# Fused RWKV-5 attention and SwiGLU block: spreading feed-forward pieces over the last attention steps, and one later silu product

## The chip, the core and the metric

The kernel runs on one core of one Trainium2 chip. The metric is the device time of one execution in microseconds (us). A run's time is that of the whole execution; the profile's span runs from the first to the last instruction.

## The reference, cut to what matters

```python
# attention: B, H, S, D = 4, 8, 768, 48
for t in range(S):
    cur = einsum('bhd,bhe->bhde', u * k[t], v[t])
    y[:, :, t] = einsum('bhd,bhde->bhe', r[t], state + cur)
    state = w * state + einsum('bhd,bhe->bhde', k[t], v[t])
x = y.transpose(0, 2, 1, 3).reshape(3072, 384)
# feed-forward: d_model 384, d_ff 1536
g = x @ w_gate
val = x @ w_val
out = (g / (1 + exp(-g)) * val) @ w_out
```

Everything is float32.

## The kernel before, in words

**Attention steps.** The 768 positions of each of 4 batches are cut into 6 chunks of 128, which makes N = 24 attention steps. Step `s` of the main loop (L1049) prepares block s and finishes older ones. `scale_k`, `scale_r` and `own_product` run on GpSimd. `move_blocks(s + 1)` puts 16 DMAs of 32 KB on SP's queue (L364), which permute the 32x32 blocks of the next step's keys and rows. `turn_blocks(s)` transposes what such DMAs brought, with two stream transposes on VectorE (L379, kT and rT). `scores(s - 1)` is 16 matmuls (L393) whose results VectorE copies through a mask (L398, two copies, the second put off in `lazy`). `outputs(s - 2)` is 56 matmuls (L426) and a copy on ScalarE (L430), and `update(s - 2)` is 32 matmuls (L441) and two sums on VectorE (L453). From step 12 on scores, outputs and update stand one after the other. In even steps from 14 to 22 `scale_r(s + 1)` comes only after `turn_blocks(s)`.

**Feed-forward pieces.** The feed-forward work of pairs of token blocks is queued in `todo` as closures, "pieces", and `feed(n)` takes n of them. `gaps(s, n)` is called at five places of each step, n = 0 to 4 (before the scores, after the attention matmuls, after the turn, near the end, at the end), and decides how many pieces go there; `turn_blocks` feeds one more between its two transposes, which `gaps` takes off at n = 1. Every engine works its instructions off in program order. So the position of a piece fixes what stands in front of what in the queue of TensorE, VectorE, ScalarE, GpSimd and SP.

**The passes of 3x3 products.** The gate and value products of g = 2, 4, 6 are made by `three_beside(g)` beside attention, in a fast multiplication scheme that works on three feature blocks at a time. There are four triples, t = 0 to 3. Each has 15 rounds of matmuls (L720, four matmul records each in the profile), which write PSUM chains named n, y, l4, l5, l1, l2, l8. Only four PSUM banks exist for them, so a round that reuses a chain waits until ScalarE or VectorE has read it (copies and sums recorded at L744). Its 60 rounds, with all that follows them on other engines, are cut into 26 pieces: the first three hold one round, the others about two and a half. When a triple is complete its silu is made: an activation on ScalarE (L751), then a product with the values, for feature blocks 0 and 1 on VectorE and for block 2 on GpSimd (all L744). `at` numbers say when: z = 15 t is the triple's first round, so z + 16.2 is just after round 1 of the next triple, and z + 22.1 just after its round 7. The values of triples 0, 2 and 3 lie in the same rows of `hv` (`place`), those of triple 1 in others. The last pieces of a pass overlap with `two_projections`, 14 items that multiply by w_out in seven products of quarters (L539, `project`), with sums on VectorE (`h_sums`, L512 to L516).

After the loop the passes for g = 8 and 10 run without attention (`three_units`, L854), and then their projections.

Of the kernel before, what the change touches and what calls it, by code (L numbers as in the profile page):

```python
# [22 lines left out]
def fast(  # L23
# [68 lines left out]
    def take():  # L92
        return free.popleft()
# [130 lines left out]
    def round_weights():  # L224
        if done["act"] > done["pool"]:
            round_pool()
        round_act()
# [390 lines left out]
    def in_place(t):  # L618

        f = 3 * t  # L620
        w = [[wgv[:, :, c, P * (f + i) : P * (f + i + 1)] for c in range(CC)] for i in range(3)]
        return [
            lambda o=o, x=x, op=op: op(o, o, x) for o, x, op in (
                (w[1][1], w[0][1], pool.tensor_add), (w[1][1], w[1][2], pool.tensor_sub),
                (w[0][0], w[1][0], pool.tensor_add), (w[0][0], w[0][2], pool.tensor_sub),
                (w[2][2], w[2][0], pool.tensor_sub), (w[2][2], w[1][2], pool.tensor_sub),
            )
        ]

    def w_forms(g, t):  # L630

        f = 3 * t
        made = wide["u", g, t] = {}

        w = [[wgv[:, :, c, P * (f + i) : P * (f + i + 1)] for c in range(CC)] for i in range(3)]
        def place():
            if t == 0 or g < THREES:
                ring = three.tile([P, 6, 2, P], FP32, name="s", tag="w_bits")
                s = [ring[:, n] for n in range(6)]
            else:  # L640
                s = (early + spare)[6 * t - 6 : 6 * t]
                s = [x.rearrange("p (o t) -> p o t", o=2) for x in s]
            made.update(zip(("r2", "r3", "r13", "r11", "r5", "r9"), s))
            made.update({
                "r0": w[1][1], "r1": w[0][1], "r4": w[0][0], "r6": w[1][2], "r7": w[2][2],
                "r8": w[1][0], "r10": w[2][0], "r12": w[0][2], "r14": w[2][1],
            })

        def form(o, a, b, op):
            op(made[o], made[a], made[b])  # L650

        return [place] + [
            lambda x=x: form(*x) for x in (
                ("r2", "r14", "r6", pool.tensor_sub), ("r3", "r8", "r1", pool.tensor_sub),
                ("r13", "r12", "r10", pool.tensor_add), ("r9", "r2", "r13", pool.tensor_sub),
                ("r9", "r9", "r7", pool.tensor_sub), ("r5", "r3", "r13", pool.tensor_sub),
                ("r5", "r5", "r4", pool.tensor_sub), ("r11", "r3", "r2", pool.tensor_sub),
                ("r11", "r11", "r0", pool.tensor_add),
            )
        ]  # L660
# [49 lines left out]
    def three_step(g, t, n, rounds, open_):  # L710

        what, chain = rounds[n]
        names = [c for _, c in rounds]
        first = n == names.index(chain)
        if first:
            wide[chain] = open_(chain)
        u, v = wide["u", min(g, THREES), t][what], wide["v", g][what]
        ps = wide[chain][:].rearrange("p (o i t) -> p o i t", o=2, i=2)
        for o in range(2):
            pe.matmul(  # L720
                ps[:, o], u[:, o], v,
                start=first and o == 0, stop=True, skip_group_check=True,
            )
# [11 lines left out]
    def three_beside(g):  # L735

        todo = []
# [4 lines left out]
        def later(at, do, out, *args):  # L742
            def run():
                do(out, *(pair_of(wide[a][:]) if isinstance(a, str) else a for a in args))  # L744
            todo.append((at, run))

        def give(at, chain):
            todo.append((at, lambda: free.append(wide.pop(chain))))

        def silu(at, then, gate, value, on):  # L750
            todo.append((at, lambda: act.activation(gate, gate, AF.Silu)))  # L751
            later(then, on.tensor_mul, gate, gate, value)

        for t in range(4):
            z = 15 * t
            rounds = ENDING if t == 3 else BESIDE
            at = {what: z + n + 0.5 for n, (what, _) in enumerate(rounds)}
            for n in range(15):
                todo.append((
                    z + n,  # L760
                    lambda t=t, n=n, r=rounds: three_step(g, t, n, r, lambda _: take()),
                ))
            if t < 3:
                forms = w_forms(g, t + 1)
                if g == FIRST and t < 2:
                    forms += in_place(t + 2)
                start = z - 4 if t else 0
                todo += [
                    (start + (z + 10 - start) * n / len(forms) + 0.15, do)
                    for n, do in enumerate(forms)  # L770
                ]
            place = NR + (6 if t == 1 else 0)
            values = hv[:, place : place + 6].rearrange("p (j i) t -> p j i t", j=2)
            gates = [[j * FC + 3 * t + i for i in range(3)] for j in range(2)]
            c = []
            for k in range(6):
                i, j = divmod(k, 2)
                row, other = gates[j][i], place + 3 * j + i
                low, high = hv[:, row], hv[:, other]
                c.append(bass.AP(  # L780
                    tensor=low.tensor, offset=low.offset,
                    ap=[list(low.ap[0]), [high.offset - low.offset, 2], [1, 2 * P]],
                ))
            later(at["r10"], act.copy, c[5], "n")
            later(at["r14"], act.copy, c[4], "y")
            later(at["r12"], act.copy, c[0], "l4")
            later(at["r13"], dve.tensor_add, c[4], c[4], "n")
            later(at["r2"], dve.tensor_add, c[5], c[5], "y")
            later(at["r9"], dve.tensor_sub, c[4], c[4], "l4")
            give(at["r9"] + 0.1, "l4")  # L790
            later(at["r5"], act.copy, c[1], "n")
            later(at["r5"] + 0.1, dve.tensor_sub, c[0], c[0], "n")
            give(at["r5"] + 0.2, "n")
            later(at["r11"], act.copy, c[2], "y")
            later(at["r11"] + 0.1, act.copy, c[3], "y")
            give(at["r11"] + 0.2, "y")
            later(at["r6"], dve.tensor_add, c[3], c[3], "l5")
            later(at["r3"], dve.tensor_add, c[2], c[2], "l1")
            later(at["r1"], dve.tensor_add, c[0], c[0], "l2")
            later(at["r7"], dve.tensor_add, c[5], c[5], "l5")  # L800
            give(at["r7"] + 0.1, "l5")
            later(at["r4"], dve.tensor_sub, c[1], "l1", c[1])
            give(at["r4"] + 0.1, "l1")
            later(at["r0"], dve.tensor_sub, c[2], c[2], "l2")
            give(at["r0"] + 0.1, "l2")
            later(at["r8"], dve.tensor_sub, c[1], c[1], "l8")
            later(at["r8"] + 0.1, dve.tensor_add, c[3], c[3], "l8")
            give(at["r8"] + 0.2, "l8")
            if t < 3:
                for i, on in enumerate((dve, dve, pool)):  # L810
                    silu(
                        *((z + 11.7, z + 11.8) if i == 2 else (z + 15.6 + i / 10, z + (22.1 if i and t < 2 else 16.2 + i / 10))),
                        hTs[:, :, 3 * t + i], values[:, :, i], on,
                    )
            else:
                for j in range(2):
                    start = (at["r0"] + 0.2, z + 14.8)[j]
                    silu(
                        start, (z + 13.9, 1e9)[j], hTs[:, j, 9:12],
                        values[:, j], dve,  # L820
                    )
# [91 lines left out]
    todo = []  # L913
# [32 lines left out]
    def gaps(s, n):  # L946

        if s not in EARLY:
            if n == 0:
                share[0] = min(-(-len(todo) // (4 - (s - 9) % 4)), 14)  # L950
            feed(share[0] // 5 + (n < share[0] % 5) - (n == 1 and BLOCKS <= s < N))
            return
        for what in EARLY[s][n]:
            if what == "R":
                if done["pool"] < NW:
                    round_weights()
                elif len(summed) < 4:
                    weight_sum()
            else:
                feed(1, 3)  # L960

    share = [0]
# [86 lines left out]
    for s in range(4, N + 2):  # L1049
# [11 lines left out]
        if s < BLOCKS:  # L1061
            turn(s)
        gaps(s, 0)
        if 4 <= s - 1 < N:
            while small:
# [459 lines left out]
```

## Time and profile before

| what | us |
|---|---|
| runs | 608.59, 605.59, 608.40 |
| median of the runs | 608.4 |
| the profiled execution, whole | 605.01 |
| its span | 603.2 |
| TensorE busy | 587.1 |
| VectorE busy | 405.6 |
| GpSimd busy | 313.3 |
| ScalarE busy | 228.2 |

The profiled execution took 1.8 us more than its span and lies 3.4 us under the median of the runs. The granted TensorE clock is 1.000 over the whole span. Busy time of TensorE is an upper bound of its work: matmuls are pipelined, and their ends are modelled. A wait therefore shows best as the time from the start of one row of matmuls to the start of the next, against its usual pace: in this trace 0.216 us for each matmul of L720 and 0.163 us for each of L539.

Scores of the loop's steps 18 to 24 start at 288, 321, 350, 379, 391, 410 and 426 us; the three passes of `three_beside` end at about 219, 311 and 406 us.

### The profile page before, as it was taken

How to read it: one execution, taken by the hardware profiler on the slowest of the kernel's cores; microseconds unless marked ns; L12 is line 12 of the kernel's file. 1: busy time of each engine (PE TensorE's matmuls, PEld its weight loads, DVE VectorE, ACT ScalarE, POOL GpSimd, SP SyncE). 2: the span in 40 equal slices, each digit the busy share in tenths (PEclk: the TensorE clock that was granted, in tenths of full speed). 3: DMA queues.
4: the chain of work that ended last, by engine and by line, in shares of the span. 5: the costliest groups of instructions: out<-in, count | busy, mean ns of one | idle time of the engine just before them, and what ended most of it. 6: DMA issues, size and time to landing. Idle time of an engine off the chain costs nothing.

```text
span 603.2 us, 12420 instructions
## 1 busy us (share of the span) xinstructions
PE 587.1 (97%) x4920; PEld 528.0 (88%) x4920; DVE 405.6 (67%) x682; ACT 228.2 (38%) x524; POOL 313.3 (52%) x349
## 2 busy tenths in 40 slices
PE   8799999999999999999999999989999999999996
PEld 7678888899888889988799988879988899988896
DVE  5867886369478877478877477959347686277660
ACT  3368887331353412253331334523234420243310
POOL 4879889988999402977701967632435200011000
PEclk9999999999999999999999999999999999999999
DMA  7989883231530503133150404121100000000001
GB/s 173 232 213 253 214 300 75 52 64 42 113 49 8 94 4 72 39 64 56 21 89 14 100 2 75 17 45 26 41 14 0 2 1 26 27 1 1 2 1 58
DMA packets 138004, 40.43 MB, mean 67 GB/s; under 512 B 128592, under 2 KB 131792, under 8 KB 137936
## 3 DMA queue, kind: packets, MB, share of 16 engines
q1 hardware_dynamic: 134480, 34.82, 27.3%
q10 hardware_dynamic: 3456, 4.72, 2.2%
q8 instruction: 41, 0.67, 0.5%
q14 instruction: 27, 0.22, 0.1%
HBM read 28.51 MB, written 4.72 MB: 55 GB/s over the span
## 4 chain that ended last, share of the span: by engine, by line
PE 83%; DVE 3%; POOL 3%; SPq 2%; ACT 1%; issue 1%; DMA 1%; DVEq 0%; POOLq 0%; ACTq 0%
PE bank L720 27%; PE bank L539 26%; PE bank L464 7%; PE c_l L720 6%; PE y_ps L426 5%; PE c_n L720 3%; PE c_y L720 3%; PE s_ps L393 3%; DVE hv L744 2%; SPq L364 2%; POOL wgv L222 1%; PE u_ps L441 1%; PE tp L349 1%; DMA r_ld<-in_r_dram 1%; ACT hv L751 0%
## 5 line engine op out<-in xcount | busy, mean ns | idle before, releaser
L744 DVE TENSOR_TENSOR hv<-hv,bank 128x512 f32<-128x512 f32 x132 | 87.2, 682 | 30.5 <-PE bank L720 17.6
L720 PE MATMUL bank<-xf,wgv 128*128 128x256 f32 x256 | 65.9, 381 | 1.7 <-DVE hv L744 1.7
L464 PE MATMUL bank<-xT,wgv 128*128 128x256 f32 x288 | 66.8, 385 | 0.6 <-ACT xT L430 0.6
L860 POOL TENSOR_TENSOR hv<-At,hats 128x512 f32<-128x512 f32 x8 | 10.2, 1274 | 107.0 <-ACT At L859 107.0
L328 ACT ACTIVATE At<-ident,du 128x128 f32<-128x128 f32 x176 | 60.0, 397 | 15.2 <-DVE du L240 8.5
L744 ACT COPY hv<-bank 128x512 f32<-128x512 f32 x72 | 40.2, 585 | 55.2 <-PE bank L720 49.1
L464 PEld LDWEIGHTS bank<-xT,wgv 128*128 128x128 f32 x288 | 53.2, 190 | 8.9 <-ACT xT L430 0.8
L720 PEld LDWEIGHTS bank<-xf,wgv 128*128 128x128 f32 x256 | 48.0, 190 | 8.9 <-DVE hv L744 2.1
L650 POOL TENSOR_TENSOR s<-wgv 128x256 f32<-128x256 f32 x39 | 29.7, 785 | 43.8 <-PE bank L539 43.7
L539 PE MATMUL bank<-wo,hv 128*128 128x192 f32 x288 | 49.5, 327 | 0.0
L539 PEld LDWEIGHTS bank<-wo,hv 128*128 128x128 f32 x288 | 47.3, 190 | 0.5
L398 DVE COPY_PREDICATED At<-mask,s_ps 128x512 f32<-128x512 int32 x48 | 34.2, 743 | 18.4 <-ACT At L328 10.0
L454 POOL TENSOR_TENSOR Z<-Z,w 48x192 f32<-48x192 f32 x32 | 17.3, 539 | 51.2 <-DVE Z L453 50.0
L539 PE MATMUL bank<-wt,hs 128*128 128x192 f32 x240 | 42.1, 328 | 0.7 <-DVE hs L513 0.6
L539 PE MATMUL bank<-wo,hs 128*128 128x192 f32 x240 | 42.4, 326 | 0.0
L545 ACT COPY hv<-bank 128x192 f32<-128x192 f32 x36 | 11.3, 316 | 78.6 <-PE bank L539 78.6
L539 PEld LDWEIGHTS bank<-wt,hs 128*128 128x128 f32 x240 | 39.2, 190 | 1.7 <-issue 1.3
L539 PEld LDWEIGHTS bank<-wo,hs 128*128 128x128 f32 x240 | 39.6, 190 | 0.2
L751 ACT ACTIVATE hv<-hv 128x512 f32<-128x512 f32 (+1 forms) x33 | 21.2, 667 | 47.7 <-DVE hv L744 47.5
L720 PE MATMUL bank<-xT,s 128*128 128x256 f32 x152 | 36.0, 382 | 1.0 <-DVE hv L744 0.7
L426 PE MATMUL y_ps<-At,v_ld 128*32 128x128 f32 x768 | 34.9, 273 | 1.3 <-DVE At L398 1.3
L720 PE MATMUL bank<-xT,wgv 128*128 128x256 f32 x144 | 35.9, 382 | 0.0
(203 smaller groups left out, 1302.4 us busy)
## 6 DMA issues: line engine op xcount, KB each, us to landing
hats<-hats SPq DMA_DIRECT2D x192, 32.0 KB, 2.0
w_bits<-in_moe_w_gate_dram SPq DMA_DIRECT2D x6, 768.0 KB, 6.9
v_ld<-in_v_dram SPq DMA_DIRECT2D x48, 96.0 KB, 3.4
w_bits<-in_moe_w_val_dram SPq DMA_DIRECT2D x6, 768.0 KB, 6.0
w_bits<-in_moe_w_out_dram SPq DMA_DIRECT2D x6, 768.0 KB, 6.4
out_dram<-hv ACTq DMA_DIRECT2D x24, 192.0 KB, 1.9
k_ld<-in_k_dram SPq DMA_DIRECT2D x20, 192.0 KB, 3.3
r_ld<-in_r_dram SPq DMA_DIRECT2D x20, 192.0 KB, 3.8
```

What stands on the lines that cost most here:

```text
L328: lambda h=h: act.activation(At[i % 2][:, h, :], ident[:], AF.Identity, scale=du[:, h : h + 1])
L364: sp.dma_start(out=bass.AP(tensor=dst.tensor, offset=dst.offset, ap=[list(dst.ap[0]), [-P, 2 * HP], [1, 32]],), in_=bass.AP(tensor=src.ten ...
L393: pe.matmul(ps[e][:, a, :], kT[i % 2][rows, at(i, a), :], turned[i][rows, at(i, a), :], start=True, stop=True, skip_group_check=True,)
L398: lazy.append(lambda e=e: dve.copy_predicated(At[i % 2][:].rearrange("p (a e) t -> p a e t", e=2)[:, :, e], mask[:].bitcast(INT32).unsquee ...
L426: pe.matmul(ps[32 * q : 32 * q + 32, cc, :], *x, start=start, stop=stop, skip_group_check=True,)
L454: pool.tensor_mul(ze, ze, w)
L464: pe.matmul(gv[:, o, :].rearrange("p (i t) -> p i t", i=2), wt[:, c, P * f : P * (f + 1)], xT[:, 2 * g % NX : 2 * g % NX + 2, c, :], start ...
L539: pe.matmul(ps, lhs[:, f, :], rhs[:, f, :], start=(f == 0 and n in (0, 1, 4)), stop=(f == FH - 1), skip_group_check=True,)
L650: op(made[o], made[a], made[b])
L720: pe.matmul(ps[:, o], u[:, o], v, start=first and o == 0, stop=True, skip_group_check=True,)
L744: do(out, *(pair_of(wide[a][:]) if isinstance(a, str) else a for a in args))
L751: todo.append((at, lambda: act.activation(gate, gate, AF.Silu)))
```

## The change

Two edits, both in the building of the order; no operation is added or taken away.

```diff
@@ three_beside, silu of triples 0 to 2
-  *((z + 11.7, z + 11.8) if i == 2 else (z + 15.6 + i / 10, z + (22.1 if i and t < 2 else 16.2 + i / 10))),
+  *((z + 11.7, z + 11.8) if i == 2 else (z + 15.6 + i / 10, z + (16.2, 22.1)[i])),
@@ gaps
-  share[0] = min(-(-len(todo) // (4 - (s - 9) % 4)), 14)
+  if s < 18:
+      share[0] = min(-(-len(todo) // (4 - (s - 9) % 4)), 14)
+  else:
+      share[0] = -(-(len(todo) + (14 if s < 21 else 0)) // max(25 - s, 1))
```

The first edit concerns triple 2 alone: its second feature block's product goes from z + 16.3 to z + 22.1, where those of triples 0 and 1 were already. The second changes how many pieces a step gets:

| step s | 18 | 19 | 20 | 21 | 22 | 23 | 24 |
|---|---|---|---|---|---|---|---|
| before | 14 | 14 | 14 | 3 | 7 | 7 | 6 |
| after | 10 | 10 | 10 | 6 | 10 | 10 | 9 |

Steps up to 17 keep theirs. The pieces keep their order among themselves, so what changes is where the attention work of steps 18 to 24 stands between them. Counted along TensorE (r a round, P a projection product, A the attention matmuls of one step), from step 17 to the end of the loop's pieces:

```
before  A17 r18 A18 r17 P r2 P5 A19 P5 r P r P2 r9 A20 r30 A21 r10 A22 r7 P r2 P2 A23 P7 A24 P4
after   A17 r15 A18 r20 P r2 A19 P10 A20 r P r P2 r11 A21 r15 A22 r25 A23 r5 P r2 P6 A24 P7
```

## The prediction

> **What bounds the kernel now.** I read the page first, then a table of windows, then the timelines of TensorE, VectorE, SP and GpSimd around each place where a row of matmuls starts late.
>
> ```profile
> span 603.2 us, 12420 instructions
> ...
> PE 587.1 (97%) x4920; PEld 528.0 (88%) x4920; DVE 405.6 (67%) x682; ACT 228.2 (38%) x524; POOL 313.3 (52%) x349
> ```
>
> TensorE is the bound. The change moves no work off it, so it can only add or remove waits of TensorE. In the part that the change reaches, the windows table leaves little of that:
>
> ```profile
> 196.00:226.00 30.00, 29.24 (x234) 25.58 (x233) 23.79 (x34) 9.75 (x22) 8.20 (x10) 1.00 0.29 49
> 284.00:316.00 32.00, 31.07 (x241) 27.19 (x240) 25.08 (x36) 12.27 (x27) 13.69 (x15) 1.00 0.32 52
> ...
> 378.00:402.00 24.00, 22.28 (x250) 18.66 (x249) 18.24 (x30) 9.27 (x22) 11.41 (x13) 1.00 0.20 31
> ```
>
> (Columns: window, its length, busy time of PE, PEld, DVE, ACT, POOL, clock, DMA share, GB/s.) VectorE, the third figure, is busy for 76 to 79% here. TensorE's timeline shows where it waits; these are the last triples of the three passes:
>
> ```profile
> 203.10 2.11 PE L720 MATMUL bank<-xf,s 128*128 128x256 f32 x8
> 205.07 3.23 PE L720 MATMUL bank<-xT,s 128*128 128x256 f32 x12
> 208.14 1.03 PE L720 MATMUL bank<-sgs,wgv 128*128 128x256 f32 x4
> ...
> 297.40 1.89 PE L720 MATMUL bank<-xf,s 128*128 128x256 f32 x8
> 299.45 1.10 PE L720 MATMUL bank<-xT,s 128*128 128x256 f32 x4 [0.17 <-ACT hv L744]
> 301.28 1.99 PE L720 MATMUL bank<-xT,s 128*128 128x256 f32 x8 [0.73 <-DVE hv L744]
> ...
> 397.58 1.03 PE L720 MATMUL bank<-xf,wgv 128*128 128x256 f32 x4
> 400.33 1.13 PE L720 MATMUL bank<-xf,wgv 128*128 128x256 f32 x4 [1.72 <-DVE hv L744]
> ```
>
> Each start is held against the pace of 0.216 us per matmul. Pass 1: 8 matmuls from 203.10 end at 204.83, the next come at 205.07 (0.24 late); 12 from 205.07 end at 207.66, the next come at 208.14 (0.48). Pass 2: 299.45 is 0.32 late, 301.28 is 0.97 late. Pass 3: 400.33 is 1.89 late. By the same reckoning 390.30 is 0.26 late. At 0.163 us per matmul of L539, 315.21 is 0.19 late, and 224.13 is 0.78 late (for hs, L513). Three more starts after 260 us are about 0.2 late each. What holds TensorE is VectorE's queue:
>
> ```profile
> 202.77 2.88 DVE L744 TENSOR_TENSOR hv<-hv 128x512 f32<-128x512 f32 x2 [0.78 <-ACT hv L751]
> 205.58 1.87 DVE L744 TENSOR_TENSOR hv<-hv,bank 128x512 f32<-128x512 f32 x3
> ...
> 297.07 2.96 DVE L744 TENSOR_TENSOR hv<-hv 128x512 f32<-128x512 f32 x2
> 299.96 0.70 DVE L379 STREAM_TRANSPOSE rT<-hats 128x512 f32<-128x512 f32 x1
> 300.58 1.84 DVE L744 TENSOR_TENSOR hv<-hv,bank 128x512 f32<-128x512 f32 x3
> ...
> 398.99 0.71 DVE L379 STREAM_TRANSPOSE kT<-hats 128x512 f32<-128x512 f32 x1 [1.84 <-DMA hats<-hats]
> 399.62 1.85 DVE L744 TENSOR_TENSOR hv<-hv,bank 128x512 f32<-128x512 f32 x3
> ```
>
> In passes 1 and 2 the two silu products of triple 2 (`hv<-hv`, x2) stand in front of the sums that free chains n and y for rounds r5 and r11. In pass 3 the sums stand behind the transpose of step 22, which waits 1.84 us for its DMAs. These come from one row of SP's queue:
>
> ```profile
> 386.43 10.97 SPq L364 DMA_DIRECT2D hats<-hats  x16
> ```
>
> They start when step 21's transposes end (386.37) and land 2.0 us after the last issue (page, part 6): about 13 us from transpose to transpose. Between them TensorE had step 22's attention and few pieces; step 21 gets 3.
>
> **The change part by part.** Attention of one step costs TensorE 1.09 + 1.68 + 0.41 = 3.2 us (chain; 2.8 without update, from step 22 on), a round 0.863, a projection product 1.95. VectorE pays per step 2 masked copies (0.74), 2 transposes (0.70), 2 sums of L453 (0.35) and a reduction (0.55).
>
> *The moved product, pass 1.* The order around pass 1 is otherwise unchanged. A product took 1.44 us there (2.88 / 2). Without the second, the three sums start at 204.14, the first has read its bank at about 204.8, and r5, due at 205.9, waits for nothing: 0.48 goes. The 0.24 before r9 stays mostly, because ScalarE's copy of l4 overwrites values that the first product reads. I count -0.5. The product now follows r5's sum (208.09 to 208.78). VectorE's gap there is 0.42, and then 0.24, 0.17 and 0.18; a product of 0.69 is absorbed in about four sums. New is a wait on ScalarE: triple 3 writes its values into the rows of triple 2, so r11's two copies (from 208.34) wait for the product, until about 209.5. Behind them is chain y, whose bank is taken again only for r8, seven rounds later, and r3's sum, due at 210.14, to which a copy ending at 210.1 just comes in time. Cost 0. From the other side, up to 0.5 per pass if r4 or r0 slip with the sums; and not a gain, since nothing is taken away there.
>
> *Pass 2, both edits.* Attention 18 moves from four rounds before triple 3 to seven before it. I walk VectorE's queue from the start of A18 = 0. Masked copy 1.3 to 2.05, sums of L453 to 4.1 (as at 289.40 and 291.41 in the trace), the sums of r6, r3, r1 to 6.7, second masked copy 7.4, kT 8.1, r7 and r4 to 9.5, rT 10.2, r0 and two sums of r8 to 12.2. Then the one product left. With 1.48 us, as at 297.07, it ends at 13.7, and ScalarE's l4 copy (0.58) at 14.3. r9 is due at 3.2 + 12 x 0.863 = 13.6 and comes 0.7 late; r5's sum ends at 14.4, before r5 is due. So 1.29 becomes 0.7 (between 0 with an undisturbed product of 0.69, and 1.0). The 0.19 at 315.21 goes too: A19 now stands between round r8 and the products that need hs, which gives VectorE and ScalarE 3.2 us. Sum -0.8.
>
> [...] The row first, min/median/max ns:
>
> ```profile
> L744 DVE TENSOR_TENSOR hv<-hv x24: 677/951/1561, 173.3 to 411.0; 128x512 f32<-128x512 f32 x18, 128x768 f32<-128x768 f32 x6
> ```
>
> Products of 128x512 take 0.69 alone and 1.44 to 1.48 while GpSimd works. [...] I take the row, 1.48. At the product's new place GpSimd is idle in passes 1 and 2 (no GpSimd row from 205.1 to 216.25, nor from 300.9 to 324.9), so both give 0.69.
>
> *Pass 3, the even shares.* Step 21 has 6 pieces, and between A21 and A22 stand 15 rounds, 12.9 us. The same walk from A21 = 0: kT at 4.1, rT ends at 8.2, 16 issues to 19.3, landed at 21.3. kT of step 22 comes up at A22 + 6.9 = 16.1 + 6.9 = 23.0: 1.7 us in time. The stall of 1.89 goes. So does about half of the 0.26, its second product being gone. Steps 18 to 20 are thinned from 14 to 10 pieces, which is still over 20 us each, against 13. Late next is VectorE, since attention now stands right before two triple boundaries. A22 stands after round 13 of triple 1: masked copies, kT, the product (1.04, or 1.48) and rT come before r13's sum, which ends at 10.0 to 10.4 after A22, while r5 is due at 9.8. I take 0.5 (0 to 0.9). A21, two rounds before triple 1: 0.15 (0 to 0.3). At the pass's end A23 no longer stands between r8 and the hs products, as it did at 410 us, so the pattern of 315.21 returns: 0.2 (0 to 0.8, as at 224.13). Sum -1.9 - 0.1 + 0.85 = -1.15.
>
> *Costed at nothing:* ScalarE's diagonals (8 x 0.4 per step, at 38% load), covered by its idle time, at most 0.3 per step without that; the loads of k, r, v on SP behind the 16 DMAs, needed a step later; GpSimd's forms for the pass g = 8, ready 5 us before 439 us in the trace and followed by two more products than needed.
>
> Total -0.5 - 0.8 - 1.15 = -2.45, say -2.5: span 600.7, the profiled execution 605.0 - 2.5 = 602.5. The median of the runs lies 3.4 above the profiled one for no reason that the trace shows, so I carry that over: 608.4 - 2.5 = 605.9.
>
> **The rivals.** *B, everything fits.* VectorE absorbs the moved attention, as it did before around A20 and A21 (345 to 378 us: TensorE 33.0 of 33.0). All the waits named go except the 0.78 at 224.13: 0.72 + 1.29 + 0.19 + 1.89 + 0.26 = 4.35, so 604.0. Against it, VectorE had no slack at the boundaries of passes 2 and 3.
>
> *C, the waits change places.* The upper ends hold: 0.24 and 1.0 stay, 0.9 + 0.3 + 0.26 + 0.8 in pass 3, and 0.5 for the late product in two passes: 4.5 of 4.35 given back. 608.5, no change. The late product's copies on ScalarE speak for it; for the first two triples such a product stood there without a stall.
>
> *D, slower.* The place is step 20. GpSimd's forms for pass 3 wait for the product 06 to free their buffer (before: the idle 5.94 ahead of 332.55). Behind them now queue `scale_k(21)` and `own_product(21)`, four forms, A20's Z products, two forms, and only then `scale_r(21)`, on which SP's 16 DMAs wait. My walk from A20: scale_r ends at 10.3, DMAs land at 23.3, kT of step 21 comes up at 24.4. Slack 1.1 us, and beyond it each us of lateness stalls TensorE by about one us (1.84 gave 1.89). If the nine forms take 1.45 each (the longest seen, at 408.87) instead of 0.78, and the three others 1.5 instead of 1.0, that is 7.5 late, a stall of 6.4 and 605.9 + 6.4 = 612.3. It turns slower than before at 3.6 late. For it: own_product did take 1.46 at 377.63. Against it: GpSimd's mean form is 0.78.
>
> **How the numbers follow.** The likeliest case has 0.60, B 0.18, C 0.15, D 0.07. About 0.5% (3 us) is what a measurement of this kernel can tell from no change. The likeliest case runs from -1.5 to -3.5, so a third of it, 0.22, passes 0.5%; with B that makes faster 0.40, D gives slower 0.07, same is 0.53. The range reaches from 602.0, B less 2.0 because the runs before fell up to 2.8 under their median, to 609.0, C and a little.
>
> **What would show it.** Right: no idle ahead of kT (L379) by DMA; one `hv<-hv` product, not two, ahead of r13's sum in each last triple; TensorE's starts late by under 1 us everywhere from 196 to 440 us, the largest behind A22 and before r9 in pass 2; TensorE's busy work unchanged. Wrong: a wait of L379 for DMA at step 21, a wait of TensorE for ScalarE's r11 copies, or TensorE idle ahead of the pass at 439 us.

## The result, and the profile after

| | before | after |
|---|---|---|
| median of six runs each, one chip | 606.68 us | 602.27 us |
| range of the runs | 605.46 to 608.59 | 602.09 to 603.55 |
| the profiled execution, whole | 605.01 | 602.26 |
| its span | 603.2 | 600.4 |

The kernel became faster: ratio 0.9926, 95% interval [0.9903, 0.9950]. The profiled executions differ by 2.8 us, the medians by 4.4. The runs of before lie in two groups, near 605.5 and near 608; what the upper group is turned out to be the other half of this case. Of the runs below, four single ones took 950 us or more (one of e5, one of e10, two of before); they are in the medians, but in no ratio and no count.

The page of the kernel after, first and second line:

```profile
span 600.4 us, 12410 instructions
...
PE 586.4 (98%) x4920; PEld 528.0 (88%) x4920; DVE 404.7 (67%) x682; ACT 227.8 (38%) x524; POOL 312.7 (52%) x349
```

The 4920 matmul records are the same, busy time moved by under 1 us, and the span fell by 2.8: what went is waiting. The windows table of the kernel after, same stretches and columns as before, shows where:

```profile
196.00:226.00 30.00, 29.37 (x236) 25.96 (x235) 23.87 (x36) 9.84 (x22) 8.18 (x9) 1.00 0.29 50
284.00:316.00 32.00, 32.00 (x334) 28.18 (x333) 24.25 (x38) 13.62 (x31) 14.68 (x17) 1.00 0.39 62
378.00:402.00 24.00, 24.00 (x171) 20.64 (x170) 17.29 (x28) 9.25 (x21) 4.85 (x7) 1.00 0.16 24
```

TensorE, the first figure after the length, is busy for all of the second and third stretch. TensorE's timeline of the kernel after, at the same three places:

```profile
203.19 2.11 PE L720 MATMUL bank<-xf,s 128*128 128x256 f32 x8
205.16 2.83 PE L720 MATMUL bank<-xT,s 128*128 128x256 f32 x12
207.83 1.03 PE L720 MATMUL bank<-sgs,wgv 128*128 128x256 f32 x4
...
297.09 1.98 PE L720 MATMUL bank<-xf,s 128*128 128x256 f32 x8
299.04 2.83 PE L720 MATMUL bank<-xT,s 128*128 128x256 f32 x12
301.70 1.03 PE L720 MATMUL bank<-sgs,wgv 128*128 128x256 f32 x4
...
405.24 4.06 PE L539 MATMUL bank<-wo,hv 128*128 128x192 f32 x24
409.88 2.19 PE L539 MATMUL bank<-wt,hs 128*128 128x192 f32 x12 [0.57 <-DVE hs L513]
```

By the pace of 0.216 us, pass 1 comes 0.24 and 0.08 late (before 0.24 and 0.48), pass 2 comes 0.22 and 0.07 late (before 0.32 and 0.97). The row at 409.88 is new: 24 matmuls at 0.163 us from 405.24 end at 409.15, so TensorE waits 0.73 us for hs, where attention of step 23 used to stand in between. VectorE's timeline of the kernel after:

```profile
296.93 1.29 DVE L744 TENSOR_TENSOR hv<-hv 128x512 f32<-128x512 f32 x1 [0.21 <-ACT hv L751]
298.25 0.69 DVE L744 TENSOR_TENSOR hv<-hv,bank 128x512 f32<-128x512 f32 x1
...
376.24 0.69 DVE L379 STREAM_TRANSPOSE kT<-hats 128x512 f32<-128x512 f32 x1
376.86 0.65 DVE L744 TENSOR_TENSOR hv<-hv 128x512 f32<-128x512 f32 x1
377.43 0.70 DVE L379 STREAM_TRANSPOSE rT<-hats 128x512 f32<-128x512 f32 x1
378.05 1.36 DVE L744 TENSOR_TENSOR hv<-hv,bank 128x512 f32<-128x512 f32 x2
```

One product instead of two stands ahead of the sum at 298.25, and the transpose of step 22 (376.24) no longer waits for DMA. SP's queue shows why:

```profile
361.33 10.76 SPq L364 DMA_DIRECT2D hats<-hats  x16
```

The row ends at 372.1, the last of its DMAs lands some 2 us later (an estimate, from the 2.0 us that the page of before has for them), and the data is needed at 376.2.

### The profile page after: what moved, and what is told of

Its sections match the earlier page's. It is cut to its first block, busy times and chain, and to the rows that moved or that the text cites. A ratio compares the mean times of both kernels' runs of the same rounds, so it can differ in the third digit from the quotient of the medians.

```text
span 600.4 us, 12410 instructions
## 1 busy us (share of the span) xinstructions
PE 586.4 (98%) x4920; PEld 528.0 (88%) x4920; DVE 404.7 (67%) x682; ACT 227.8 (38%) x524; POOL 312.7 (52%) x349
## 4 chain that ended last, share of the span: by engine, by line
PE 88%; POOL 2%; DVE 2%; issue 1%; DMA 1%; ACT 0%; SPq 0%; DVEq 0%; POOLq 0%
PE bank L720 31%; PE bank L539 26%; PE bank L464 7%; PE c_l L720 6%; PE y_ps L426 6%; PE c_n L720 3%; PE c_y L720 3%; PE s_ps L393 3%; POOL wgv L222 1%; PE u_ps L441 1%; PE tp L349 1%; DMA r_ld<-in_r_dram 1%; DVE hv L744 1%; DVE hs L513 0%; POOL hats L310 0%
## 5 line engine op out<-in xcount | busy, mean ns | idle before, releaser
L328 ACT ACTIVATE At<-ident,du 128x128 f32<-128x128 f32 x176 | 60.3, 396 | 15.6 <-DVE hv L552 7.5
```

What stands on the lines that cost most here:

```text
L328: lambda h=h: act.activation(At[i % 2][:, h, :], ident[:], AF.Identity, scale=du[:, h : h + 1])
```

## The experiments

Two questions: do the two edits bring what the prediction's steps said, each at its own place, and why do the medians differ by more than the profiles?

### One edit at a time: e1_silu_only, e2_shares_only, e3_before_again

e1 is before with the first edit alone, e2 is after with the first edit taken back, e3 is before unchanged.

```diff
 e2, against after
-  z + (16.2, 22.1)[i]
+  z + (22.1 if i and t < 2 else 16.2 + i / 10)
```

> The kernel before with the first edit alone: triple 2's second silu product later, the shares untouched. Waits theory (the gain is the named waits of TensorE, one by one): in pass 1 the 0.48 us before r1 goes, as it did in the changed kernel (-0.4); in pass 2 one of two products leaves the front of r13's sum, 1.29 us becomes about 0.4 (-0.9); in pass 3 the wait of about 1.9 us for the DMAs of step 22 stays. Span 603.2 - 1.3 = 601.9. Rival (the shares alone matter, the product is absorbed wherever it stands): 603.2, and TensorE still 0.9 us or more late at the end of pass 2's r5. Second question, on the spread of the runs, which were 605.5 to 605.8 and 607.6 to 608.6 before and 602.1 to 602.5 (one 603.6) after: if the wait for step 22's DMAs is what differs from run to run, this kernel keeps two groups about 3 us apart.

> The changed kernel without the first edit: even shares, but triple 2's second product back at the start of triple 3. Waits theory: pass 1 keeps its 0.72 us; pass 2 has two products before r13's sum again, so r5 or r9 is about 1.2 us late there though attention stands three rounds earlier; pass 3 loses the wait for DMAs (1.89) and has about 0.74 before the products that need hs, as in the changed kernel, and about 0.3 at the start of triple 3. Span about 603.2 - 1.5 = 601.7; with the silu edit alone the two gains sum to the 2.8 us of both. Rival (moving attention away from triple 3 already frees VectorE, the edits overlap): pass 2 is as in the changed kernel, 0.3 late, and the span 600.9. On the spread: without the wait for step 22's DMAs the runs should lie within 0.5 us of each other, if that wait is the cause of the two groups.

> The kernel before, unchanged, for a second profile and for its spread. The two sets of medians differ by 4.4 us, the two profiled executions by 2.7. Theory: the kernel before has executions of two kinds, about 605.5 and 608.4, the profile shown was of the faster kind, and the slower kind has a longer wait for DMAs at step 22; then five more runs show both kinds, and a profile of the slower kind would show the idle time of VectorE ahead of the transpose L379 at 3 to 5 us instead of 1.84. Rival: the slower kind loses its 3 us elsewhere (in the first 60 us, where weights are loaded, or spread over all rows), and the profile shows step 22 unchanged.

| | median, us | ratio to before | span |
|---|---|---|---|
| e1 | 603.8 | 0.9959 [0.9944, 0.9974] | 602.1 |
| e2 | 603.24 | 0.9952 [0.9938, 0.9966] | 601.4 |
| e3 | 607.2 | 1.0013 [0.9996, 1.0030] | 603.3 |

By spans the first edit is worth 1.2 us, the second 1.9, both together 2.9 (from 603.3): nearly a sum. Lateness of TensorE, read as above, in us:

| | before | e1 | e2 | after |
|---|---|---|---|---|
| pass 1, end of the 12 (or 8 + 4) behind r9 | 0.48 | 0.07 | 0.48 | 0.08 |
| pass 2, r9 and behind it | 1.29 | 0.40 | 0.72 | 0.29 |
| pass 3, DMA wait of step 22 | 1.89 | 1.81 | 0 | 0 |
| end of pass 3, hs | 0 | 0 | 0.73 | 0.73 |

Pass 1 belongs to the product alone. In pass 2 the first edit alone takes away 0.89 of 1.29 and the second 0.57, but both together 1.0: the gains overlap there. e2 lies between its two expectations (1.2 and 0.3). With attention out of the way, two products in a row still cost 0.49 behind r9. TensorE's timeline of e2 has 12 matmuls there, which end by the pace at 302.10, and the next row starts at 302.59:

```profile
299.51 3.24 PE L720 MATMUL bank<-xT,s 128*128 128x256 f32 x12
```

### Half a cure for the DMA wait: e4_step21_five

```diff
 against before
+  share[0] = {21: 5, 22: 7, 23: 6, 24: 5}.get(s, share[0])
```

> The kernel before with one share changed: step 21 gets 5 pieces instead of 3 (22, 23, 24 then get 7, 6, 5), which puts 15 rounds instead of 10 between the attention matmuls of steps 21 and 22; all before step 21 is untouched, the product too. Waits theory: the DMAs of step 22 need about 13 us from transpose to transpose, TensorE now has 12.9 + 3.2 us of work there, so the wait of 1.89 us goes and passes 1 and 2 keep theirs; the attention of step 23 no longer stands before the products that need hs, which costs up to 0.75. Span 603.2 - 1.9 + 0.5 = 601.8. Rival (it is the thinning of all steps from 18 on, VectorE's load per step, that helps): the wait moves to the sums after step 22 and at least 1.5 us of lateness stays in pass 3.

604.48 us, ratio 0.9971 [0.9957, 0.9985], span 602.5. The DMA wait was gone as expected, but the span fell by only 0.8. TensorE's timeline of e4 names the place where the rest went:

```profile
404.10 4.06 PE L539 MATMUL bank<-wo,hv 128*128 128x192 f32 x24
408.73 2.19 PE L539 MATMUL bank<-wt,hs 128*128 128x192 f32 x12 [0.56 <-DVE hs L513]
```

Attention of step 23 no longer stands between round r8 and the products that need hs, and 0.72 us of waiting appear. The expectation had seen this wait coming (up to 0.75) and counted 0.5 for it, so its span was 601.8. The two waits make 1.2 us (1.89 - 0.72); why only 0.7 to 0.8 of it reached the span was not tested. The run was already 0.16 us behind before's ahead of pass 3 (297.56 against 297.40, in the last triple of pass 2).

### One piece less instead: e5_step21_two

```diff
 against before
+  share[0] = {21: 2, 22: 7, 23: 7, 24: 7}.get(s, share[0])
```

> The kernel before, with 2 pieces instead of 3 in step 21 and 7 instead of 6 in step 24; all else unchanged. Between the attention matmuls of steps 21 and 22 stand 7 rounds instead of 10, 2.6 us less. Theory 1 (the wait of 1.8 us in step 22 is set by a floor of about 13 us from the transposes of step 21 to the landing of the 16 DMAs that follow them, 11 us of issue and 2 us of landing, and TensorE's work between falls short of it): the wait of VectorE's transpose for its DMA grows by about the 2.6 us taken away, to 4.4, and the span from 603.3 to about 605.9. Theory 2 (the DMAs come late for another reason, say because scale_r or the pieces ahead of them on GpSimd come at a fixed place in the order of pieces): the wait grows by less than 1 us and the span stays within 1 us of 603.3.

609.55 us, ratio 1.0041 [1.0016, 1.0066], span 606.5. VectorE's and SP's timelines of e5:

```profile
399.72 0.71 DVE L379 STREAM_TRANSPOSE kT<-hats 128x512 f32<-128x512 f32 x1 [3.20 <-DMA hats<-hats]
```

```profile
387.19 10.95 SPq L364 DMA_DIRECT2D hats<-hats  x16
```

From the first issue to the waiting transpose it is 12.5 us (399.72 - 387.19), as before (398.99 - 386.43 = 12.6): a floor that the shorter stretch of work did not move. The wait grew from 1.84 to 3.20, by 1.4 and not by 2.6: the direction of theory 1, half its size. The other half went into another wait: attention 22 now followed attention 21 so closely that VectorE stood 1.86 us for ScalarE's diagonals (L328) ahead of the masked copy at 393.38, and came up to kT 7.2 us after attention 22 began (396.52 - 389.27) instead of 5.9 (397.15 - 391.25). The span grew by more than the wait did, and that led to the clock, below.

### A version that beats both: e6_ends, with e8_after_again

```diff
 against after
+  share[0] = {14: 16, 15: 12, 22: 14, 23: 8, 24: 7}.get(s, share[0])
```

> The kernel after still waits at the ends of two passes, 0.79 us ahead of TensorE's start at 223.8 and 0.74 us ahead of the start at 409.9, both times for VectorE's hs (L513), where products of L539 follow round r8 directly. In pass 2 an attention step stands between them and only 0.15 us is left. Here the kernel after gets other shares in five steps (14: 16, 15: 12, 22: 14, 23: 8, 24: 7 pieces), so that an attention step stands between r8 and those products in passes 1 and 3 too; the order of the pieces is unchanged. Theory 1 (TensorE waits only because nothing else stands between, and an attention step's 3 us cover VectorE's sums): both waits fall to under 0.2 us, span 600.4 - 1.3 = 599.1, time some 1.3 us under the kernel after. Theory 2 (VectorE is the limit there, and attention's own VectorE work of some 3 us, the two copies through a mask, two transposes and two sums, only goes into the same queue ahead of hs): the waits move to the rounds before, or to the start after, and the time stays within 0.4 us of the kernel after.

> The kernel after, unchanged, beside the others on one chip, to measure e6_ends against it. Expected: 602.3 us, span 600.4 (both theories), runs close together.

e6: 600.6 us (600.21 to 601.37), ratio to before 0.9902 [0.9884, 0.9921], span 598.8. e8 on the same chip: 602.58 (602.36 to 603.31), ratio 0.9935 [0.9917, 0.9952], span 600.8. The six runs of each don't overlap; the medians lie 2.0 us apart. TensorE's timeline of e6, then VectorE's:

```profile
404.09 4.17 PE L539 MATMUL bank<-wo,hv 128*128 128x192 f32 x24
408.10 2.11 PE L539 MATMUL bank<-wt,hs 128*128 128x192 f32 x12
```

```profile
406.67 0.96 DVE L513 TENSOR_TENSOR hs<-hs,hv 128x768 f32<-128x768 f32 x1
```

The second row of TensorE now starts 0.1 us behind the pace and names no releaser: hs is ready at 407.6, half a microsecond early, because attention's matmuls stand before these products. VectorE is later too, since attention brings it work (hs is ready 7.3 us after round r8 starts at 400.37, in the kernel after 5.4 us), but by less than the 2.8 us that attention takes on TensorE. Theory 1 holds for both passes (pass 1: 219.06 and 223.06). The two waits and r9 of pass 3, no longer 0.22 late, make 1.5 of the 2.0 us, where 1.3 was forecast; the other 0.5 is not accounted for.

### What the upper group of before is: e7, e9 to e12

The profile of e5 has one window of TensorE's clock at 0.91 for 400 to 420 us. Cut finer, the clock is 0.50 from about 401.6 to 405.0 (the ends are estimates, from the 0.56 and 0.53 of the half microseconds there), right after a rest of TensorE of 2.60 us, which ended at 401.06. That suggested that the runs of before near 608 are those in which the clock is halved behind the rest ahead of 400.3. e7, e11 and e12 are before unchanged, for a profile of such a run. e9 and e10 fill the rest with work that changes nothing:

```diff
 three_step; k is 3 in e9, 2 in e10
-  for o in range(2):
+  for o in range(2) if (g, t, what) != (6, 3, "r6") else (0, 1) * k:
```

> The kernel before, with the matmuls of round r6 in the last triple of pass 3 issued three times instead of once; the last pass over them writes the same numbers into the same bank again. They stand just ahead of TensorE's wait of 1.5 to 1.8 us (the start at 400.3), and two repeats are 8 matmul records of 0.216 us, 1.73 us: they fill the wait with work and nothing is taken off VectorE or SP. Theory 1 (the runs of before that lie 2 to 3 us above the others have TensorE's clock halved for one or two stretches of 3.4 us after this wait, as the profile of e5_step21_two shows after a longer one): VectorE's wait for DMA stays at about 1.8 us, the start at 400.3 stays, and all runs lie in the lower group, spans 603.2 to 604.2, median time 605.5, a run above 604.8 in span at most one in six. Theory 2 (the scatter has another cause): about half the runs have spans above 604.8, as in before.

> The same with one repeat, 0.86 us, so that 0.6 to 0.9 us of TensorE's wait are left. Theory 1: a rest that short is no longer than the waits of the kernel after (0.79), whose runs lie close together, so spans of 603.2 to 604.2 as in e9_fill_two. Theory 2: about half the runs above 604.8. If e9 is tight and this one is not, the length of the wait that decides lies under 0.9 us.

> The kernel before, unchanged, for a profile of a run of its upper group, of which none was caught so far. If it is one (span above 604.8): theory 1 expects a granted clock near 0.5 for 3.4 us, or twice that, right after the start near 400 us, and all other starts as in the profile before; theory 2 expects the lost time elsewhere. If it is of the lower group, nothing follows.

> The same again, for the same reason: theory 1 expects a halved clock after the start near 400 us in a run with a span above 604.8, theory 2 the lost time elsewhere.

> The kernel before, unchanged, for one more profile of it. Its runs lie in two groups near 605.5 and near 608, and the profiles so far (spans 603.2 and 603.3) belong to the lower group. Expected if the profile falls in the upper group: a span of about 606. Theory 1 (the upper group pays at one place, where a wait turns long): one start of TensorE between 196 and 440 us comes 2 to 3 us later than in the lower group. Theory 2 (a clock): the granted clock is under 1.000 and every row of matmuls is a little longer. If it falls in the lower group, it repeats the profile before within 0.2 us and nothing follows.

e7 was of the lower group (605.19 us, span 603.4). e11 is of the upper one: 607.41 us, span 605.6. Its windows (window, length, busy time of PE, clock, DMA share, GB/s), then TensorE's timeline:

```profile
401.00:402.00 1.00, 0.84 (x4) 0.98 0.00 0
402.00:403.00 1.00, 1.00 (x4) 0.50 0.00 0
403.00:404.00 1.00, 1.00 (x4) 0.50 0.00 0
404.00:405.00 1.00, 1.00 (x5) 0.50 0.26 43
405.00:406.00 1.00, 1.00 (x7) 0.81 0.34 55
```

```profile
401.16 1.32 PE L720 MATMUL bank<-xf,wgv 128*128 128x256 f32 x4 [1.99 <-DVE hv L744]
402.27 1.91 PE L720 MATMUL bank<-xT,wgv 128*128 128x256 f32 x4
403.98 2.81 PE L539 MATMUL bank<-wo,hv 128*128 128x192 f32 x12
```

Four matmuls from 402.27 take 1.71 us to the next start where 0.86 is the pace. The half clock runs from about 401.96 to 405.38, worked out from the 0.98 and the 0.81 of the two broken windows: 3.4 us, an estimate. The three rows together lose 1.8 us; 3.4 us at half clock account for 1.7 of it. That is most of the 2.4 us between 605.6 and 603.2. The wait itself was 0.3 longer in this run, and the run was 0.57 us behind ahead of it (394.59 against 394.02).

Here the clock fell after a rest of 1.99 us. But e12 rested 2.33 us at the same place and kept a clock of 1.00 (606.27 us, span 604.4):

```profile
401.56 1.13 PE L720 MATMUL bank<-xf,wgv 128*128 128x256 f32 x4 [2.33 <-DVE hv L744]
```

So whether the clock falls differs from run to run; why is not shown. There is a second, earlier stretch in e11:

```profile
20.00:30.00 10.00, 9.18 (x125) 0.85 1.22 264
```

At a clock of 0.50 it would be 3.0 us long (an estimate, from the 0.85); before has 1.00 in this window. What it cost is not shown: e12, with 1.00 from 0 to 40 us, was as far behind ahead of the wait (394.65 against 394.02).

Filling the rest tests whether it is the rest that makes the upper group. TensorE's timeline of e9:

```profile
397.67 2.75 PE L720 MATMUL bank<-xf,wgv 128*128 128x256 f32 x12
401.13 1.13 PE L720 MATMUL bank<-xf,wgv 128*128 128x256 f32 x4 [0.71 <-DVE hv L744]
```

| same chip | runs with a span over 604.8 | median, us | ratio to before |
|---|---|---|---|
| before | 9 of 22 | 606.2 | |
| e9, rest 0.7 us in the profiled run | 1 of 12 | 605.57 | 0.9982 [0.9967, 0.9998] |
| e10, rest 1.0 us | 0 of 11 | 605.75 | 0.9990 [0.9975, 1.0004] |

VectorE still waits for its DMA (2.6 and 2.0 us), so that wait alone does not make the upper group. With TensorE's rest filled, 1 of 23 runs was long, against 9 of 22. The mean granted clock of each run says too that the upper group is a matter of the clock: of the 22 of before in the table, the nine long ones have 0.992 to 0.996, the thirteen others 0.995 to 1.000. A stretch of 3.4 us at 0.50 takes 0.003 off this mean (an estimate, 1.7 of 605 us); e11, with two stretches, has 0.993, so the lowest runs probably had more than one. Needless matmuls, 1.7 us of them, did not make the kernel slower, and its median a little shorter.

Two things stay open. e1 keeps the rest (1.65 us) and yet had 1 run of 10 some 2 us above the others, where before on that chip had 10 of 30, and 7 of 12 in e3. And single long runs come without that rest too: one of ten in e2 (605.03 us, clock 0.996), one of twelve in e9 (608.24 us, clock 0.995). Where these lost their time is not on record; a stretch near the start, as in e11, is a rival.

## Why the prediction was right, and where it was not

It said 602.5 us for the profiled execution; 602.26 was measured. It said 605.9 for the median; 602.27 was measured, inside the range by 0.3, and faster by over 0.5% where "same" had the larger chance. So most steps of the sum held, and one step behind the sum failed. Luck had a part in both numbers. The first is so close because two errors in pass 3 cancelled, below. The second lies in the range only because 2.0 us had been taken off case B for the scatter of the runs; the likeliest case, 605.9, missed it by 3.6. Of these, 1.7 are the starting point (608.4, the median of three runs, against 606.68 of six), and 1.9 the gain, 4.4 instead of 2.5. (Among the chances, a third of 0.60 is 0.20 and not 0.22.)

**The carried offset failed.** The step "the median of the runs lies 3.4 above the profiled one for no reason that the trace shows, so I carry that over" took the upper group for something that the change leaves alone. In the main it belongs to the wait that the change removes: TensorE's rest of 1.9 us, and in e11, the one long run of before with a profile, a stretch of half clock behind it, which cost about 1.7 us (long runs of before: 10 of 30, 9 of 22 and 8 of 13 on three chips). With the rest gone the offset goes too: after's median lies 0.01 above its profiled run. The sign was there to see: three runs in two groups, and a profile from the lower one. The median's extra 1.6 us (4.4 - 2.8) fits that share, but its size is not shown: filling the rest in e9 and e10 took 0.6 and 0.4 us off the median.

**Pass 1**, -0.5: -0.40, the 0.24 before r9 staying as said. The late product took 0.68 at 208.39, and VectorE absorbed it; r11's copies held up nothing.

**Pass 2**, -0.8: -1.04, in the row at 299.04 and behind it 0.29 of 1.29 left, where 0.7 was forecast. The walk put the product at A18 + 12.2 with 1.48 us; it started at 11.7 (296.93 - 285.2) with 1.29. Half a microsecond of VectorE's queue was counted too much. At the pass's end 0.15 of 0.19 stayed, though attention stands in between. The prediction ties the 1.44 to 1.48 us of a product to GpSimd's work; but in the profile of before three products took 0.68 to 0.69 beside GpSimd rows too (178.77, 189.82 and 195.02). At the moved product's new place in passes 1 and 2, with no GpSimd row, it took 0.68 as forecast (208.39 and 302.26 in the kernel after).

**Pass 3**, -1.15: -1.2, but from other terms. The DMA wait went (-1.89), with about 2.1 us of slack (376.24 against 374.1) where 1.7 was worked out. Behind A22 (0.5) and A21 (0.15) nothing was lost: the product there, counted with 1.04 or 1.48, took 0.65 (376.86), so the sum of r13 was done at about 378.7, 9.1 after A22, and r5, due 9.8 after it, did not wait. The half of the 0.26 did not go: 0.22 stays (391.69), with a single product of 0.69 there. Against that, hs was put at 0.2 (0 to 0.8) and cost 0.73. A term of 0.65 that was not there and one of 0.53 that was missing cancelled.

**Sum:** -0.40 - 1.04 - 1.2 = -2.6 of the 2.8 that the spans show.

**Rivals.** B counted 4.35 gained; what it lacks is mostly r9, still 0.22 to 0.24 late in all three passes, and the hs wait. C, where waits change places, was seen once, at hs, and e4 shows the same exchange alone: 1.89 us gone, 0.72 new. The largest lateness left is that of hs, 0.78 us at 223.82 and 0.73 at 409.88, and not behind A22 or before r9, where the prediction looked for it. D did not come: scale_r(21) ended 10.4 us after A20 (343.35 - 332.97; 10.3 walked), the DMAs followed at 343.37 and step 21's kT ran at 357.39 without waiting for them; the forms behind A20 took 0.72 to 0.79 each. But it was close: the row of DMAs took 11.64 us, to 355.01, and in before the waiting transpose came 1.6 us behind the end of such a row (398.99 - 397.40), so the data was there at about 356.6, an estimate, 0.8 us ahead.

## What to carry to other kernels

When runs of one kernel fall into two groups, don't treat the gap as noise that every version inherits: look up which group the profile is from, and look at the granted clock behind the rests of the bounding engine. In e11 a rest of TensorE of 1.99 us had 3.4 us at a clock of 0.50 behind it, some 1.7 us on top of the wait; in e12 a rest of 2.33 us had none. And when work is moved out of one place, look first at what it was covering there: attention matmuls between a round and the products that need its sums hid 0.7 us of VectorE work, and putting them back at two such places (e6) came with another 2 us, 1.3 of them at these two places.

## What the runs showed of the hardware that was not expected

- A rest of TensorE of 1.99 us (e11) and one of 2.60 us (e5) were followed by 3.4 us at a granted clock of 0.50, some 1.7 us lost (an estimate, half of 3.4). Rests of 2.33 us (e12) and 1.72 us (the profile of before) were not, each in one profiled run. e11 also has a clock of 0.85 from 20 to 30 us. With the rest cut to 0.71 us (e9) and 0.96 us (e10), in the profiled runs, 1 of 23 runs was long.
- VectorE's products of two SBUF operands, 128x512, took 0.65 to 0.69 us at their new places. The one that stayed ahead of r9 took 1.48, 1.29 and 0.69 us in the last triples of the three passes.
